# Attention with a soft mixture of experts: the sums of the weights by seven TensorE streams of a quarter of the queries per column group

## The chip, the cores and the metric

The kernel runs on one core of one Trainium2 chip. The time is the device time of one execution in microseconds; the lower the better. The engines named below are TensorE (PE, matrix products; PEld its weight loads), VectorE (DVE), ScalarE (ACT), GpSimd (POOL) and SyncE (SP, which issues the transfers, SPq).

## What is computed

Rotary attention over 8 batches of 8 heads, 576 positions, 64 channels a head, and then a soft mixture of 8 experts with 4 slots each over the 4608 tokens of 512 channels:

```python
q_rot, k_rot = rotate(q), rotate(k)
scores = scale * q_rot @ k_rot.T
attn = exp(scores - scores.max(-1))
attn = attn / (attn.sum(-1) + 1e-9)
x = (attn @ v)                       # as (4608, 512)
logits = x @ phi                     # (4608, 32)
d = softmax(logits, axis=0)          # over the tokens
slots = d.T @ x                      # 32 slots
out = softmax(logits, axis=1) @ (relu(slots @ w1[e]) @ w2[e])
```

The change concerns `attn.sum(-1)`, the sums of the weights.

## The kernel before, in words

Two heads make a pair, held in the two halves of the 128 partitions; there are 32 pairs, four to a batch. The weights of a pair (`exp` of the scores) are computed transposed, keys in the partitions and queries along the row, in nine blocks of 64 keys: `t0` to `t8`, each a TensorE product of 16 matmuls into a bank pair of the accumulator `s_ps` and a ScalarE exponential out of it (lines 220, 221). Blocks 2j and 2j+1 go to tile `a_t` j, block 8 to `a_rem`. Half the partitions of a block hold one head, half the other, and the halves change place between the first and the second 288 queries. `av0` to `av8` (line 236) multiply the values by the weights into `o_ps`, and `o_out` copies that to `xt` on ScalarE.

Ahead of that, for each pair: `load0`, `load1` bring queries and keys, `spin0`, `spin1` multiply by cosines and sines on GpSimd (line 140), `join` adds on VectorE (line 144), `high0`, `high1` cast on ScalarE, `low` takes the remainder on VectorE (line 153), `m00` to `m31` and `m_rem` find the maxima of the scores (matmuls of line 173, VectorE maxima of line 175), `m_min`, `m_turn`, `m_half`, `m_rows` turn them into a row that `t0` to `t8` subtract.

Behind it come the sums. On VectorE `add1` adds `a_t` 0 and 1 into `c_t` (line 253), `add2` adds `a_t` 2, `add3` adds the second half of `a_t` 3 (line 255). `total` (line 265) then lets TensorE sum over the partitions: four terms (the two halves of `c_t`, `a_rem`, the first half of `a_t` 3), each in a column group of its own, for each half of the queries. `total_out` copies the four partial sums to `s4` on ScalarE (line 270), `send` moves them by four transfers to `rc`, 12 queries per partition (line 276), `recip` adds the four on VectorE (line 282) and takes reciprocals, `spread` and `widen` bring them over DRAM to all partitions, and `norm` multiplies `xt` by them on GpSimd (line 299). The last two pairs go another way (`sums_turn`, `sums_wide`, `norm_wide`): TensorE turns and widens the sums. `logits`, `natural` and, once per batch, the slot sums and the softmax over slots follow two beats later; the experts come at the end.

The order of all this is written out by a table of numbers, `WHEN`: a task's number is its place in units of a quarter beat, counted from the start of its pair's beat; beat p runs all tasks sorted by their place modulo 4, each for the pair that is due. Each engine then runs its instructions in exactly that order. All TensorE results but `o_ps` go through a rotation of three bank pairs of `s_ps` (`bank2`), so a product waits until the one three places before it has been read.

Of the kernel before, what the change touches and what calls it, by code (L numbers as in the profile page):

```python
# [44 lines left out]
RC = 12  # L45
PIECE = 4
WHEN = {
    "load0": -15.9, "load1": -14.496, "spin0": -13.466, "spin1": -12.4, "join": -9.9, "high0": -9.4817, "high1":
    -9.0595, "low": -8.0, "m01": -6.5262, "m10": -5.894, "m00": -5.0601, "m11": -4.7, "load_v": -3.85, "m20": -3.771,
    "m21": -3.317, "m30": -2.9, "m31": -2.7, "m_rem": -2.6642, "m_min": -2.49, "m_turn": -1.744, "m_half": -1.667,  # L50
    "m_rows": -1.545, "t0": 0.0, "weights": 0.144, "t1": 0.2, "trickle0": 0.55, "step0": 0.5949, "t2": 1.024, "av0":
    1.159, "t3": 1.1844, "av1": 1.448, "step1": 1.516, "trickle1": 1.55, "t4": 1.9121, "t5": 1.9131, "av2": 2.25,
    "trickle2": 2.55, "add1": 2.9224, "t6": 3.0, "av3": 3.157, "av4": 3.163, "step2": 3.169, "av5": 3.179, "t7": 3.3708,
    "trickle3": 3.55, "av6": 3.6564, "t8": 3.7429, "step3": 3.7743, "add2": 4.0014, "av7": 4.504, "av8": 4.5085,
    "o_out": 4.52, "add3": 4.6009, "total": 5.54, "total_out": 5.55, "send": 5.56, "sums_turn": 6.0, "sums_wide": 6.3,
    "norm_wide": 6.4, "logits_late": 7.0, "logits_sum_late": 7.05, "recip": 7.294, "natural_late": 7.3, "spread": 7.31,
    "natural_out_late": 7.35, "widen": 7.3768, "norm": 8.706, "logits": 10.54, "logits_sum": 10.579, "stats": 11.3708,
    "natural": 11.52, "natural_out": 11.536,
# [5 lines left out]
def attn_softmoe(ctx, tc, qk, v, phi, w1, w2, cs, ident, sel, seg, out):  # L64
# [30 lines left out]
    bits = const.tile([P, 5], F32, name="bits")  # L95
    ones, warm, tiny, fold = bits[:, 0:1], bits[:, 1:2], bits[:, 2:3], bits[:, 3:5]
# [8 lines left out]
    pick = const.tile([P, NS + 1], F32, name="pick")  # L105
    nc.gpsimd.memset(pick, 0.0)
    for h in (0, 1, 2):
        nc.gpsimd.memset(pick[rows[h % 2], h:h + 1], 1.0)

    nc.vector.memset(tiny, 0.0)  # L110
    nc.vector.memset(tiny[0:32], 1e-9)
# [51 lines left out]
    def bank2():  # L163
        return ps_s.tile([P, 2, 512], F32, name="s_ps")
# [83 lines left out]
    def add(p, j):  # L248
        if j == 1:
            cts[p] = att.tile([P, 2, S], F32, name="c_t")  # L250
        c, a = cts[p], ats[p, j]
        if j < 3:
            nc.vector.tensor_tensor(out=c, in0=c if j > 1 else ats[p, 0], in1=a, op=ALU.add)  # L253
        else:
            nc.vector.tensor_tensor(out=c[:, 1], in0=c[:, 1], in1=a[:, 1], op=ALU.add)  # L255

    sg = {}
    rcs = [const.tile([96, 4, RC], F32, name=f"rc{i}") for i in range(2)]

    def total(p):  # L260
        c, r, a = cts.pop(p), rems[p], ats[p, 3]
        sg[p] = s = bank2()
        for n in range(2):
            for i, m in enumerate((c[:, 0], c[:, 1], r, a[:, 0])):
                nc.tensor.matmul(s[32 * i:32 * i + 32, n, 0:HC], lhsT=pick[:, n:n + NS], rhs=m[:, half[n]],  # L265
                                 start=True, stop=True, tile_position=(0, 32 * i))

    def total_out(p):
        s, s4 = sg[p], late.tile([P, S], F32, name="s4", bufs=1)
        nc.scalar.activation(out=s4.rearrange("p (n x) -> p n x", n=2), in_=s[:, :, 0:HC], func=AF.Identity, bias=tiny)  # L270
        sg[p] = s4

    def send(p, eng):
        s4, rc = sg.pop(p), rcs[p % 2]
        for i in range(4):
            eng.dma_start(out=rc[:, i, :], in_=s4[32 * i:32 * i + 2])  # L276
# [3 lines left out]
    def recip(p):  # L280
        rr = small.tile([P, RC], F32, name="rr", bufs=2)[0:96]
        nc.vector.tensor_reduce(out=rr, in_=rcs[p % 2].rearrange("p k x -> p x k"), axis=AX.X, op=ALU.add)
        nc.vector.reciprocal(out=rr, in_=rr)
        sg[p] = rr

    def spread(p, eng):
        rr = sg.pop(p)
        rd = dram.tile([2, S], F32, name="r_row")
        eng.dma_start(out=rd.rearrange("h (r x) -> (h r) x", x=RC), in_=rr)
        sg[p] = rd  # L290

    def widen(p, eng):
        rd = sg.pop(p)
        rbs[p] = rb = late.tile([P, S], F32, name="rb", bufs=1)
        for h in range(2):
            eng.dma_start(out=rb[rows[h]], in_=rd[h:h + 1].broadcast_to([64, S]))
# [4 lines left out]
    def sums_turn(p):  # L301
        s4 = sg.pop(p)
        t = bank2()
        for j in range(5):
            w = P if j < 4 else 64
            nc.tensor.matmul(t[0:w, 0, 2 * j:2 * j + 2], lhsT=s4[:, P * j:P * j + w], rhs=fold, start=True, stop=True)
        rn = small.tile([P, RC], F32, name="rr", bufs=2)
        nc.vector.reciprocal(out=rn[:, 0:8], in_=t[:, 0, 0:8])
        nc.vector.reciprocal(out=rn[0:64, 8:10], in_=t[0:64, 0, 8:10])
        sg[p] = rn  # L310

    def sums_wide(p):
        rn = sg.pop(p)
        sg[p] = t = bank2()
        for j in range(5):
            w = P if j < 4 else 64
            for h in range(2):
                nc.tensor.matmul(t[rows[h], j // 4, P * (j % 4):P * (j % 4) + w],
                                 lhsT=rn[0:w, 2 * j + h:2 * j + h + 1].broadcast_to([w, 64]), rhs=id_sb[0:w, 0:w],
                                 start=True, stop=True)  # L320

    def norm_wide(p):
        t, xt = sg.pop(p), xts[p]
        nc.vector.tensor_tensor(out=xt[:, 0:512], in0=t[:, 0], in1=xt[:, 0:512], op=ALU.mult)
        nc.vector.tensor_tensor(out=xt[:, 512:S], in0=t[:, 1, 0:64], in1=xt[:, 512:S], op=ALU.mult)

    def natural(p):
        b, pp = divmod(p, NP)
        if pp == 0:
            xns[b] = xp.tile([P, 5, DM], F32, name="xn")  # L330
        xt = xts[p]
        flat["n"] = t = bank2()
        for j in range(4):
            nc.tensor.transpose(t[:, 0, j * P:(j + 1) * P], xt[:, j * P:(j + 1) * P], id_sb)
        nc.tensor.transpose(t[0:64, 1, 0:P], xt[:, 512:576], id_sb)

    def natural_out(p, copy=nc.scalar.copy):
        b, pp = divmod(p, NP)
        xn, t = xns[b], flat.pop("n")
# [3 lines left out]
    def logits(p):  # L343
        b, pp = divmod(p, NP)
        xt = xts[p]
        flat["l"] = lp = bank2()[:, 0]
# [7 lines left out]
    def logits_sum(p):  # L354
        b, pp = divmod(p, NP)
        lp, lb = flat.pop("l"), l_sb[:, b % 2, :]
# [183 lines left out]
    def fast(task):  # L540
# [19 lines left out]
        "add2": lambda p: add(p, 2),  # L560
        "add3": lambda p: add(p, 3),
# [66 lines left out]
    nc.vector.memset(fold, 0.0)  # L628
    for i in range(0, P, 32):
        nc.vector.tensor_copy(out=fold[i:i + 2], in_=id_sb[i:i + 2, i:i + 2])  # L630
# [40 lines left out]
    while pending:  # L671
        step(p)
    release_stk()
    for name in ("add1", "add2", "av4", "av5", "add3", "av6", "av7", "av8", "o_out", "total", "total_out"):
        do(name, p)
# [258 lines left out]
```

## Time and profile before

| what | us |
|---|---|
| three executions | 609.35, 609.97, 616.3 |
| their median | 609.97 |
| span of the profiled execution, first to last instruction | 611.8 |

Of the profiled execution the span is the time that is known; it lies 1.8 us over the median of the three. It falls into a start (to about 45 us, until the first products with the values), 31 beats of about 15 us, one a pair, and a tail (from about 527 us: the last pair's sums, the slots, the experts' weights and the output). What the views below show is read by place: a row of a timeline has its start and its length in us, the engine, the line of the code, the operation, the tiles written and read, and how many instructions it holds.

### The profile page before, as it was taken

How to read it: one execution, taken by the hardware profiler on the slowest of the kernel's cores; microseconds unless marked ns; L12 is line 12 of the kernel's file. 1: busy time of each engine (PE TensorE's matmuls, PEld its weight loads, DVE VectorE, ACT ScalarE, POOL GpSimd, SP SyncE). 2: the span in 40 equal slices, each digit the busy share in tenths (PEclk: the TensorE clock that was granted, in tenths of full speed). 3: DMA queues.
4: the chain of work that ended last, by engine and by line, in shares of the span. 5: the costliest groups of instructions: out<-in, count | busy, mean ns of one | idle time of the engine just before them, and what ended most of it. 6: DMA issues, size and time to landing. Idle time of an engine off the chain costs nothing.

```text
span 611.8 us, 23277 instructions
## 1 busy us (share of the span) xinstructions
PE 532.9 (87%) x10064; PEld 352.1 (58%) x10064; DVE 497.0 (81%) x729; ACT 326.9 (53%) x647; POOL 315.1 (52%) x308
## 2 busy tenths in 40 slices
PE   3668999998999899989999899898898999799981
PEld 2346666656765566666656565666566666443551
DVE  6879899999998999999998999999899874322341
ACT  2145656665665565656656566565465655324441
POOL 2668498655676566647763857658654000100000
PEclk9679999999999999999999999999899999859996
DMA  7153555555555555555555555455542246649999
GB/s 260 60 195 119 175 174 173 174 174 173 174 173 174 174 174 174 173 175 174 174 173 175 173 174 174 174 174 174 171 141 62 64 130 206 206 142 350 349 376 298
DMA packets 71734, 111.63 MB, mean 182 GB/s; under 512 B 20176, under 2 KB 47568, under 8 KB 71632
## 3 DMA queue, kind: packets, MB, share of 16 engines
q1 hardware_dynamic: 71618, 110.15, 54.5%
q8 instruction: 79, 1.29, 0.9%
q14 instruction: 23, 0.19, 0.1%
q10 hardware_dynamic: 14, 0.00, 0.0%
HBM read 99.93 MB, written 9.58 MB: 179 GB/s over the span
## 4 chain that ended last, share of the span: by engine, by line
PE 35%; DVE 26%; DMA 20%; ACT 6%; SPq 5%; issue 5%; POOL 1%; DVEq 0%; ACTq 0%
PE s_ps L220 8%; PE o_ps L236 8%; DVE nm L175 7%; DMA rc<-s 7%; DMA w_exp<-in_w 6%; DVE c_t L253 6%; DVE hl L153 5%; SPq L276 4%; ACT a_t L221 3%; PE s_ps L265 3%; DMA x_in<-in_qk 3%; PE s_ps L773 3%; DMA v_in<-in_v 2%; DVE c_t L255 2%; PE s_ps L173 2%
## 5 line engine op out<-in xcount | busy, mean ns | idle before, releaser
L140 POOL TENSOR_TENSOR x_in<-x_in,cs_sb 128x288 f32<-128x288 f32 x248 | 264.9, 1101 | 63.0 <-DMA x_in<-in_qk 38.1
L221 ACT ACTIVATE a_t<-s_ps 128x576 f32<-128x576 f32 x256 | 158.9, 649 | 97.8 <-PE s_ps L220 95.9
L175 DVE TENSOR_REDUCE nm<-s_ps 128x2 f32<-128x576 f32 x256 | 187.1, 743 | 15.1 <-PE s_ps L173 14.9
L236 PE MATMUL o_ps<-a_t,v_in 64*64 64x288 f32 x2048 | 172.4, 413 | 1.0 <-ACT xt L244 0.3
L220 PE MATMUL s_ps<-hl 64*64 64x288 f16 x3456 | 155.5, 286 | 16.4 <-DVE nm L175 15.9
L220 PEld LDWEIGHTS <-hl 64*64 64x64 f16 x3456 | 104.4, 107 | 59.9 <-issue 43.8
L299 POOL TENSOR_TENSOR xt<-xt,rb 128x576 f32<-128x576 f32 x30 | 42.8, 1425 | 141.0 <-DMA rb<-r_row 104.1
L173 PE MATMUL s_ps<-hl 64*64 64x288 f16 x1024 | 82.1, 298 | 26.0 <-DVE nm L175 20.5
L220 PE MATMUL s_ps<-peak,lift 64*64 64x288 f16 x1152 | 89.1, 284 | 0.0
L236 PEld LDWEIGHTS o_ps<-a_t,v_in 64*64 64x64 f32 x2048 | 72.9, 133 | 21.0 <-issue 7.3
L173 PEld LDWEIGHTS <-hl 64*64 64x64 f16 x1024 | 45.0, 107 | 49.1 <-issue 37.7
L149 ACT CAST hl<-x_in 128x576 f16<-128x576 f32 (+1 forms) x66 | 40.1, 650 | 33.1 <-DVE x_in L144 30.3
L270 ACT ACTIVATE s<-s_ps,bits 128x576 f32<-128x576 f32 x32 | 23.7, 740 | 58.0 <-PE s_ps L265 26.3
L144 DVE TENSOR_TENSOR x_in<-x_in 128x1152 f32<-128x1152 f32 (+2 forms) x36 | 53.4, 1483 | 0.5 <-POOL x_in L140 0.4
L253 DVE TENSOR_TENSOR c_t<-c_t,a_t 128x1152 f32<-128x1152 f32 x32 | 51.6, 1611 | 0.0
L153 DVE TENSOR_TENSOR hl<-x_in,hl 128x1152 f16<-128x1152 f32 x32 | 49.5, 1546 | 1.8 <-ACT hl L149 1.8
L253 DVE TENSOR_TENSOR c_t<-a_t 128x1152 f32<-128x1152 f32 x32 | 50.6, 1582 | 0.0
L220 PEld LDWEIGHTS <-lift 64*64 64x64 f16 x1152 | 38.1, 108 | 0.6
L265 PE MATMUL s_ps<-c_t,pick 128*32 128x288 f32 x256 | 37.1, 411 | 0.0
L265 PE MATMUL s_ps<-a_rem,pick 128*32 128x288 f32 x128 | 36.9, 411 | 0.0
L265 PE MATMUL s_ps<-a_t,pick 128*32 128x288 f32 x128 | 36.9, 411 | 0.0
L221 ACT ACTIVATE a_rem<-s_ps 128x576 f32<-128x576 f32 x32 | 20.8, 651 | 17.0 <-PE s_ps L220 17.0
(183 smaller groups left out, 597.6 us busy)
## 6 DMA issues: line engine op xcount, KB each, us to landing
x_in<-in_qk SPq DMA_DIRECT2D x62, 576.0 KB
w_exp<-in_w SPq DMA_DIRECT2D x63, 512.0 KB
v_in<-in_v SPq DMA_DIRECT2D x32, 576.0 KB
rb<-r_row SPq DMA_DIRECT2D x60, 144.0 KB
out<-w_exp SPq DMA_DIRECT2D x16, 512.0 KB
rc<-s SPq DMA_DIRECT2D x120, 4.5 KB
x_in<-in_qk SPq DMA_DIRECT2D x4, 288.0 KB
out<-w_exp SPq DMA_DIRECT2D x4, 256.0 KB
```

The lines of the kernel that those rows point to most:

```text
L140: eng.tensor_tensor(out=x[:, :, c], in0=x[:, :, c], in1=cs_sb[:, :, c], op=ALU.mult)
L144: nc.vector.tensor_tensor(out=x[:, t, 0, c], in0=x[:, t, 0, c], in1=x[:, t, 1, c], op=ALU.add)
L149: nc.scalar.copy(out=halves[p][:, 1 + t, c], in_=loaded[p][:, t, 0, c])
L153: nc.vector.tensor_tensor(out=hl[:, 0:4:3], in0=x[:, :, 0], in1=hl[:, 1:3], op=ALU.subtract)
L173: nc.tensor.matmul(s[rows[c], h, 0:HC], lhsT=hl[rows[h], QH, at:at + D], rhs=hl[rows[h], KH, half[n]], start=True, stop=True)
L175: nc.vector.tensor_reduce(out=nms[p][:, n, j:8:4], in_=s[:, :, 0:HC], axis=AX.X, op=ALU.max, negate=True)
L220: nc.tensor.matmul(s[rows[h ^ n], n, 0:HC], lhsT=lhs, rhs=rhs, start=(i == 0), stop=(i == 3))
L221: nc.scalar.activation(out=weights_of(p, b).rearrange("p (n x) -> p n x", n=2), in_=s[:, :, 0:HC], func=AF.Exp, scale=SCALE)
L236: nc.tensor.matmul(o[rows[h], n, 0:HC], lhsT=vt[r, b, n], rhs=a[r, half[n]], start=(b == 0), stop=(b == KB - 1))
L253: nc.vector.tensor_tensor(out=c, in0=c if j > 1 else ats[p, 0], in1=a, op=ALU.add)
L265: nc.tensor.matmul(s[32 * i:32 * i + 32, n, 0:HC], lhsT=pick[:, n:n + NS], rhs=m[:, half[n]], start=True, stop=True, tile_position=(0, 32 ...
L299: eng.tensor_tensor(out=xts[p], in0=xts[p], in1=rbs.pop(p), op=ALU.mult)
```

## The change

`add2` and `add3` go; `add1` stays. `total` takes seven terms in place of four: the two halves of `c_t`, the four halves of `a_t` 2 and 3, and `a_rem`. The four column groups now hold four quarters of the queries (144 each), and the seven terms are added up in the accumulator. So `s4` is 128 x 144, holds finished sums, and one transfer brings them to `rc`; `recip` takes reciprocals alone. The last two pairs' way is cut to the new layout (4 executed turns in place of 10, one multiplication in place of two), and the matrix `fold`, which four VectorE copies made at the start, goes. All numbers of `WHEN` are other numbers, and the last tasks behind the loop follow the table too.

```diff
-    bits = const.tile([P, 5], F32, name="bits")
-    ones, warm, tiny, fold = bits[:, 0:1], bits[:, 1:2], bits[:, 2:3], bits[:, 3:5]
+    bits = const.tile([P, 3], F32, name="bits")
+    ones, warm, tiny = bits[:, 0:1], bits[:, 1:2], bits[:, 2:3]
...
-        if j < 3:
-            nc.vector.tensor_tensor(out=c, in0=c if j > 1 else ats[p, 0], in1=a, op=ALU.add)
-        else:
-            nc.vector.tensor_tensor(out=c[:, 1], in0=c[:, 1], in1=a[:, 1], op=ALU.add)
+        nc.vector.tensor_tensor(out=c, in0=c if j > 1 else ats[p, 0], in1=a, op=ALU.add)
...
     def total(p):
-        c, r, a = cts.pop(p), rems[p], ats[p, 3]
-        sg[p] = s = bank2()
-        for n in range(2):
-            for i, m in enumerate((c[:, 0], c[:, 1], r, a[:, 0])):
-                nc.tensor.matmul(s[32 * i:32 * i + 32, n, 0:HC], lhsT=pick[:, n:n + NS], rhs=m[:, half[n]],
-                                 start=True, stop=True, tile_position=(0, 32 * i))
+        c = cts.pop(p)
+        terms = [c[:, 0], c[:, 1]] + [ats[p, j][:, i] for j in range(N_ADD + 1, 4) for i in range(2)] + [rems[p]]
+        sg[p] = s = bank2()[:, 0, 0:QC]
+        for i, m in enumerate(terms):
+            for g in range(4):
+                n = g // 2
+                nc.tensor.matmul(s[32 * g:32 * g + 32], lhsT=pick[:, 16 * n:16 * n + NS], rhs=m[:, QC * g:QC * g + QC],
+                                 start=(i == 0), stop=(i == len(terms) - 1), tile_position=(0, 32 * g))
...
     def send(p, eng):
-        s4, rc = sg.pop(p), rcs[p % 2]
-        for i in range(4):
-            eng.dma_start(out=rc[:, i, :], in_=s4[32 * i:32 * i + 2])
+        eng.dma_start(out=rcs[p % 2], in_=sg.pop(p)[0:P:16])
...
-        nc.vector.tensor_reduce(out=rr, in_=rcs[p % 2].rearrange("p k x -> p x k"), axis=AX.X, op=ALU.add)
-        nc.vector.reciprocal(out=rr, in_=rr)
+        nc.vector.reciprocal(out=rr, in_=rcs[p % 2])
...
-        for j in range(5):
-            w = P if j < 4 else 64
-            nc.tensor.matmul(t[0:w, 0, 2 * j:2 * j + 2], lhsT=s4[:, P * j:P * j + w], rhs=fold, start=True, stop=True)
+        for u in range(2):
+            nc.tensor.matmul(t[0:HQ, 0, 8 * u:8 * u + 8], lhsT=s4[:, HQ * u:HQ * u + HQ], rhs=id_sb[:, 0:P:16],
+                             start=True, stop=True)
...
-        "add2": lambda p: add(p, 2),
-        "add3": lambda p: add(p, 3),
+        "add2": lambda p: N_ADD > 1 and add(p, 2),
...
-    nc.vector.memset(fold, 0.0)
-    for i in range(0, P, 32):
-        nc.vector.tensor_copy(out=fold[i:i + 2], in_=id_sb[i:i + 2, i:i + 2])
```

What this does to the order, engine by engine. TensorE in an ordinary beat, from the last score product ahead of the sums (line numbers shift: 265 is 267 after, 173 is 176, 220 is 223). Before:

```order
L173 MATMUL s_ps<-hl 64x288
L265 MATMUL s_ps<-c_t,pick 32x288 x2
L265 MATMUL s_ps<-a_rem,pick 32x288
L265 MATMUL s_ps<-a_t,pick 32x288
L220 LDWEIGHTS hl
```

The four rows of line 265 stand twice, once for each half of the queries. After:

```order
L176 MATMUL s_ps<-hl 64x288
L267 MATMUL s_ps<-c_t,pick 32x144 x8
L267 MATMUL s_ps<-a_t,pick 32x144 x16
L267 MATMUL s_ps<-a_rem,pick 32x144 x4
L223 LDWEIGHTS hl
```

Eight matmuls of 288 columns became 28 of 144. A little later in the same beat, before, the transpose of the maxima (line 194, `m_turn`) and the logits (348, 351) behind a product with the values (236):

```order
L236 MATMUL o_ps<-a_t,v_in 64x288 x4
L194 MATMUL s_ps<-id_sb,nm 9x128
L348 MATMUL s_ps<-xt,phi_sb 32x128 x4
L351 MATMUL s_ps<-xt,phi_sb 32x64 x4
```

And after:

```order
L239 MATMUL o_ps<-a_t,v_in 64x288 x4
L347 MATMUL s_ps<-xt,phi_sb 32x128 x4
L350 MATMUL s_ps<-xt,phi_sb 32x64 x4
L197 MATMUL s_ps<-id_sb,nm 9x128
L239 MATMUL o_ps<-a_t,v_in 64x288 x4
```

The logits moved ahead of the transpose, and a value product stands behind it. VectorE over an ordinary beat, before, from the evacuation of the logits (`l_sb`) on:

```order
L360 TENSOR_TENSOR l_sb<-s_ps,l_sb 128x192
L253 TENSOR_TENSOR c_t<-a_t 128x1152
L175 TENSOR_REDUCE nm_7258<-s_ps 128x2
L282 TENSOR_REDUCE rr<-rc_121 96x12
L283 RECIPROCAL rr<-rr 96x12
L153 TENSOR_TENSOR hl<-x_in,hl 128x2x576
L253 TENSOR_TENSOR c_t<-c_t,a_t 128x1152
L255 TENSOR_TENSOR c_t<-c_t,a_t 128x576
L187 TENSOR_REDUCE nm<-nm_7258 128x9
L144 TENSOR_TENSOR x_in<-x_in 128x2x576
```

(Maxima of line 175 stand between them.) After:

```order
L190 TENSOR_REDUCE nm<-nm_10041 128x9
L147 TENSOR_TENSOR x_in<-x_in 128x2x576
L178 TENSOR_REDUCE nm_10390<-s_ps 128x2
L255 TENSOR_TENSOR c_t<-a_t 128x1152
L359 TENSOR_TENSOR l_sb<-s_ps,l_sb 128x192
L178 TENSOR_REDUCE nm_10390<-s_ps 128x2 x2
L282 RECIPROCAL rr<-rc_120 96x12
L186 TENSOR_REDUCE nm_10390<-s_ps 128x2
L156 TENSOR_TENSOR hl<-x_in,hl 128x2x576
L178 TENSOR_REDUCE nm_10390<-s_ps 128x2 x4
```

Two of the three adds and the reduction of `rc` are gone, and the remaining add stands directly ahead of the logits' evacuation, not behind it. On ScalarE the cast `high0` now stands ahead of `m_half`; on SyncE `load1` stands behind `send`, and `m_rows` behind `load1`.

## Rows read from the trace of the kernel before

**Rows 1.** Page, part 1: busy us, share of the span and instructions of each engine

```profile
PE 532.9 (87%) x10064; PEld 352.1 (58%) x10064; DVE 497.0 (81%) x729; ACT 326.9 (53%) x647; POOL 315.1 (52%) x308
```

**Rows 2.** Timeline of ScalarE: copies of the sums; in brackets its idle time before

```profile
55.59 0.74 ACT L270 ACTIVATE s<-s_ps,bits 128x576 f32<-128x576 f32 x1 [1.62 <-PE s_ps L265]
...
471.88 0.74 ACT L270 ACTIVATE s<-s_ps,bits 128x576 f32<-128x576 f32 x1 [1.59 <-DMA v_in<-in_v]
```

**Rows 3.** Windows: length, busy of PE, PEld, DVE, ACT, POOL, TensorE clock, DMA, GB/s

```profile
55.60:471.90 416.30, 380.67 (x7937) 260.46 (x7935) 393.21 (x553) 250.03 (x491) 270.87 (x246) 1.00 0.51 167
...
471.70:485.30 13.60, 13.36 (x294) 9.28 (x291) 12.65 (x19) 8.90 (x16) 1.56 (x2) 1.00 0.24 69
485.30:500.64 15.34, 14.91 (x308) 9.79 (x305) 11.59 (x22) 8.88 (x21) 1.52 (x2) 1.00 0.38 118
...
542.50:612.00 69.50, 53.40 (x500) 26.57 (x500) 19.94 (x35) 23.84 (x50) 1.74 (x2) 0.87 0.97 319
```

**Rows 4.** Waits, 60 to 515 us: who for whom, total us, times, longest

```profile
PE s_ps L173 <- DVE nm L175: 14.2, 16, 2.1
PE s_ps L220 <- DVE nm L175: 13.2, 31, 1.4
...
DVE rr L282 <- DMA rc<-s: 7.5, 13, 1.4
```

**Rows 5.** Timeline of TensorE: transposes of a batch's logits, and what follows

```profile
504.49 0.33 PE L408 MATMUL s_ps<-id_sb,l_sb 128*128 128x128 f32 x1
...
504.86 0.47 PE L236 MATMUL o_ps<-a_t,v_in 64*64 64x288 f32 x4
```

**Rows 6.** Groups of VectorE: busy us, mean ns | idle before them, releaser

```profile
L253 DVE TENSOR_TENSOR c_t<-c_t,a_t 128x1152 f32<-128x1152 f32 x32 | 51.6, 1611 | 0.0
L253 DVE TENSOR_TENSOR c_t<-a_t 128x1152 f32<-128x1152 f32 x32 | 50.6, 1582 | 0.0
...
L255 DVE TENSOR_TENSOR c_t<-c_t,a_t 128x576 f32<-128x576 f32 x32 | 25.1, 783 | 1.4 <-ACT a_t L221 1.3
...
L282 DVE TENSOR_REDUCE rr<-rc 96x12 f32<-96x48 f32 x30 | 6.7, 224 | 7.8 <-DMA rc<-s 7.5
```

**Rows 7.** Timeline of TensorE: first two of four sets of the sums, and what follows

```profile
344.79 0.44 PE L265 MATMUL s_ps<-c_t,pick 128*32 128x288 f32 x2
...
345.06 0.41 PE L265 MATMUL s_ps<-c_t,pick 128*32 128x288 f32 x2
...
345.90 0.56 PE L220 MATMUL s_ps<-hl 64*64 64x288 f16 x12
```

**Rows 8.** Timeline of TensorE: logits (128, then 64 columns); accumulating sets of 256 columns

```profile
362.49 0.43 PE L348 MATMUL s_ps<-xt,phi_sb 128*32 128x128 f32 x8 [0.16 <-ACT a_t L221]
362.71 0.32 PE L351 MATMUL s_ps<-xt,phi_sb 128*32 128x64 f32 x8
362.96 0.32 PE L173 MATMUL s_ps<-hl 64*64 64x288 f16 x4
...
566.14 0.39 PE L797 MATMUL o_ps<-w_exp 128*32 128x256 f32 x2
...
566.36 0.39 PE L797 MATMUL o_ps<-w_exp 128*32 128x256 f32 x2
```

**Rows 9.** Waits in the ordinary beat 471.7 to 485.3

```profile
PEld s_ps L194 <- ACT a_t L221: 0.4, 1, 0.4
...
PEld o_ps L236 <- ACT xt L244: 0.4, 1, 0.4
...
PE s_ps L348 <- ACT a_t L221: 0.2, 1, 0.2
```

**Rows 10.** Timeline of SyncE's queue: the four transfers of a pair's sums

```profile
361.29 2.75 SPq L276 DMA_DIRECT2D rc<-s  x4
```

**Rows 11.** Timeline of VectorE at the start

```profile
13.11 2.86 DVE L630 COPY bits<-id_sb 2x2 f32<-2x2 f32 x4
16.00 1.42 DVE L175 TENSOR_REDUCE nm<-s_ps 128x2 f32<-128x576 f32 x2
```

## What I expect, before the result

> **What bounds the kernel now.** I read the busy shares first [rows 1]: TensorE 87%, VectorE 81%, and both fall in the tail, so a share over the whole span decides nothing. The stages do. The ScalarE copies of the sums come once per pair; the first starts at 55.59 us, that of pair 27 at 471.88 [rows 2]. So 27 steady beats take 416.3 us, 15.42 us each, and this is two thirds of the span. In that window VectorE is busy 393.2 of 416.3 us (94%, 14.56 us a beat) and TensorE 380.7 (91%, 14.10 a beat), at a full granted clock, with DMA at 0.51 [rows 3]. Both look full; which one sets the beat shows in two later beats in which GpSimd has no rotations left (busy 1.56 and 1.52 us) and VectorE runs undisturbed [rows 3]: 471.70 to 485.30 is an ordinary beat, 13.60 us, TensorE busy 13.36, VectorE 12.65; 485.30 to 500.64 holds a batch's slot sums too, 15.34 us, TensorE busy 14.91, VectorE only 11.59. There TensorE sets the beat. Of every four beats one carries slot sums, one the two transposes of a batch's logits (504.49 to 504.86, 0.37 us [rows 5]), and two neither. So a beat that TensorE alone limits is (15.34 + 13.97 + 2 x 13.60) / 4 = 14.13 us, and the 1.29 us between that and 15.42 are VectorE's doing: adds, joins and evacuations in one queue. The table of waits bears it out from TensorE's side: between 60 and 515 us, some 30 beats, TensorE's two kinds of score matmuls wait 14.2 and 13.2 us for VectorE's maxima [rows 4], 0.9 a beat. The tail from 542.50 on (DMA busy 0.97 [rows 3]) follows the attention at a fixed distance and moves with it.
>
> **The change part by part.**
>
> VectorE per beat loses the second add (1.61), the half add (0.78) and the reduction of the four partial sums (0.22) [rows 6]: 2.61 us, of 14.56 leaves 11.95. That is below any estimate of TensorE's beat, so the 1.29 us are free to go; more than them is not, because TensorE is next.
>
> TensorE's sums: 16 executed matmuls of 288 columns become 56 of 144 columns (28 in the program; every fp32 matmul runs twice, as 8 in the program are 16 in the trace). Now: four column groups run at once, a set of four starts every 0.24 us, and from the first set at 344.79 to the next work at 345.90 it is 1.11 us: four sets 0.97, change-over 0.14 [rows 7]. After: 14 sets. A 144-column set is nowhere in the trace. Nearest: two sets of 128 columns in 0.22 us, 0.11 each [rows 8], and sets of 256 columns that accumulate over terms in four column groups as the new ones do, one from 566.14 to 566.36 [rows 8]. All three come to 0.84 or 0.85 ns a column, so I take 0.12 a set: 1.68 + 0.14 = 1.82 us, 0.71 more than now. Bounds: 0.11 (the 128-column set), 0.24 (the 288-column set, as if halving brought nothing).
>
> The rows leave no room for a cost per instruction: what 128, 256 and 288 columns take is in proportion. The Trainium skill (TensorEngine Tiling (Array Packing), Instruction Overhead) says otherwise and against this change: some 60 cycles for each matmul on trn2; estimated from that page, 25 ns more for each of 14 sets, 0.35 us a beat, and the sum below would read 596.
>
> Order: the logits of an older pair now stand ahead of the transpose of the maxima (m_turn), not behind it, and the copy of the sums shrinks from 576 to 144 columns. In the ordinary TensorE-limited beat TensorE's weight load for the transpose waits 0.4 us and the logits 0.2 us for exponentials [rows 9], which themselves stand behind that 576-column copy of 0.74 us [rows 2]. Bounds: both gone (-0.6), neither (0); I take half, -0.3. The wait of the value products for the output copy (0.4 [rows 9]) stays: av8, copy and av0 keep their places.
>
> m_half moves behind the first cast (high0), which waits for VectorE's join; behind them on ScalarE stands the exponential of t6, and TensorE's next banks wait for it. On SyncE load1 moves behind the transfer of the sums and the rows of the maxima (m_rows) behind load1. I cost these at nothing: in VectorE's order join stands ahead of a maximum and the add, so it is over before the logits are evacuated, and the rotation of load1's half is due only in the next beat. If the cover is gone, the price is a wait of about the one VectorE instruction ahead, at most an add of 1.58 [rows 6] a beat; a gain I exclude, since nothing waits for these now.
>
> Transfers: four issues of 2.75 us together become one [rows 10]. VectorE's waits for them are 7.5 us in 13 times between 60 and 515 us [rows 4], part of the 1.29 already; not counted again.
>
> Start: four copies on VectorE (from 13.11 [rows 11]) go, and the first maximum (16.00) follows them with nothing in between: -2.9 us. Everything up to the first exponentials hangs on this queue; bound above 0, if GpSimd's rotation were later than the maxima.
>
> Last beats: pairs 28 to 31 are TensorE-limited already, so they pay 4 x (0.71 - 0.3) = +1.6. For the last two pairs fewer, narrower matmuls turn the sums, one of them directly behind the copy it waits for; I set this to 0, with a microsecond either way.
>
> **Sum.** A beat becomes 14.13 + 0.71 - 0.3 = 14.54 us, 0.88 less: 27 x 0.88 = -23.8. With -2.9 and +1.6 the profiled span of 611.8 becomes 586.7, 25.1 us less. The median shown, 609.97, lies 1.8 under that span; the same step down gives **585 us**.
>
> **Rivals.**
>
> *Better order:* both ScalarE waits go and the shorter copy frees more, 14.1 us a beat: 0.44 x 31 less, 571. For it: the waits named above. Against: banks are still three.
>
> *A new wait in place of the old* (nearly no change): logits and m00 share a bank of the rotation of three; logits are summed by VectorE behind the remaining add (1.58 [rows 6]), which now stands directly ahead of it, and m00 comes only four TensorE tasks later. Also m_half behind the cast. From +0.42 us a beat on (31 x 0.42 = 13) the gain falls under 2%: 598; a wait of 0.7 gives 607. For it: the rotation made such waits before; against it: VectorE has 2.6 us of slack.
>
> *A set costs more than its columns* (the other side, slower): the 64-column sets take 0.25 us for two [rows 8], 0.07 each above their columns. With that on every new set the beat has 14 x 0.07 = 0.98 more, and the time is 615, within 2%. If a 144-column set took the 0.24 us of a 288-column one, 14 x 0.12 = 1.7 a beat, 31 beats, 53 us: 638. It is slower by over 2% from 0.21 us a set on (37 us / 31 / 14 = 0.086 above 0.12). Against it: the 64-column sets are below what a set needs to be started, the 128-column ones are not, and the accumulating 256-column sets show nothing.
>
> The page's rule is a milder form of this rival (596). It needs a fixed cost that the 128- and 256-column rows don't show; 0.05 for it, within the forecast's range.
>
> That the change doesn't do what it says I exclude: the order shows the adds and three of four transfers gone in every beat.
>
> **How the numbers follow.** Forecast 0.55 (578 to 597, the page's case in it); better order 0.15 (about 571 to 578); a new wait, or a small fixed cost per set, 0.22 (598 to 615); slower through the sets 0.08 (over 622). A measurement of this kernel tells about 2% from no change, 12.2 us: faster is below 597.8, slower above 622.2. So faster 0.70, same 0.22, slower 0.08. The range: 572 to 604 leaves 0.05 below, and above it the slower case and the upper part of the new waits, 0.15.
>
> **What would show it.** Right: copies of the sums 14.5 us apart on average in steady state; starts of the sums' sets 0.12 apart, 14 of them, under 1.9 us in all; VectorE's share in the steady beats near 82%, TensorE's above 95%; VectorE's first maximum at about 13 us; one transfer of sums per pair on SyncE. Wrong: sets 0.14 or more apart; TensorE idle before m00, t7 or t0 for VectorE or a transfer; the transpose of the maxima waiting for the join; beats still at 15.

## The result, and the profile after

Four executions of the changed kernel beside four of the kernel before gave a median of 587.91 us against 611.07, a ratio of 0.962 (95% interval 0.956 to 0.969): 23 us less. The forecast was 585, in a range of 572 to 604. The span of the profiled execution is 585.4 us, 26.4 less than the 611.8 before. The sum came out; two of its terms for the beat did not, and the experiments below show which.

Page, part 1 of the kernel after (busy us, share of the span, instructions), and below it, from part 4, the share of each engine in the chain of work that ended last, first after, then before:

```profile
PE 539.7 (92%) x11356; PEld 387.5 (66%) x11356; DVE 422.7 (72%) x625; ACT 313.5 (54%) x647; POOL 298.1 (51%) x308
...
PE 85%; DVE 4%; DMA 3%; ACT 3%; issue 2%; SPq 0%; DVEq 0%; ACTq 0%
```

```profile
PE 35%; DVE 26%; DMA 20%; ACT 6%; SPq 5%; issue 5%; POOL 1%; DVEq 0%; ACTq 0%
```

Where [rows 1] had two engines near their limit, one is left: TensorE rises from 87% to 92%, VectorE falls from 81% to 72%, and the chain, which used to change between TensorE, VectorE and the transfers, now runs on TensorE almost throughout.

The copies of the sums, which [rows 2] used as the clock of the beats (name of the instruction, count, shortest/median/longest in ns, first and last start), and three windows of the kernel after (length, busy us of PE, PEld, DVE, ACT, POOL, granted TensorE clock, DMA share, GB/s), to be laid beside [rows 3]:

```profile
L272 ACT ACTIVATE s<-s_ps,bits x32: 380/380/382, 51.2 to 502.8; 128x144 f32<-128x144 f32 x32
```

```profile
51.20:446.46 395.26, 389.70 (x9017) 292.89 (x9016) 332.57 (x471) 238.23 (x490) 257.99 (x249) 1.00 0.55 177
446.46:502.78 56.32, 54.92 (x1240) 39.46 (x1232) 25.90 (x46) 30.46 (x66) 4.50 (x5) 1.00 0.42 126
...
518.28:585.40 67.12, 49.60 (x491) 25.58 (x480) 20.04 (x35) 23.29 (x48) 1.73 (x2) 0.91 1.00 329
```

The copies of pairs 0 and 27 start at 51.20 and 446.46: 27 steady beats of 14.64 us, against 15.42. In them TensorE is busy 98.6% (91% before) and VectorE 84% (94% before). The span of 26.4 us less falls apart by these marks: 4.4 ahead of the first copy (55.59 to 51.20), 21.0 in the 27 steady beats (416.3 to 395.3), 1.4 given back in the last four (54.9 to 56.3), 2.4 behind the last copy.

Waits of the kernel after between 60 and 480 us (who for whom, total us, times, longest): the largest of TensorE's own, two of its weight loads, one of VectorE:

```profile
PE s_ps L223 <- issue: 2.3, 6, 0.6
```

```profile
PEld o_ps L239 <- ACT xt L247: 9.0, 29, 0.3
PEld s_ps L333 <- ACT a_t L224: 8.3, 24, 0.3
```

```profile
DVE nm L178 <- PE s_ps L176: 52.0, 89, 2.2
```

The 14.2 and 13.2 us that TensorE's score products waited for VectorE's maxima [rows 4] are gone, and the sign has turned: VectorE now waits 52 us for score products. The weight load of the product with the values still waits 0.3 us a beat for the output copy, as the prediction left it.

The new sums on TensorE, in an ordinary beat (start, length, engine, line, what, count):

```profile
341.03 0.70 PE L267 MATMUL s_ps<-c_t,pick 128*32 128x144 f32 x16
341.54 1.16 PE L267 MATMUL s_ps<-a_t,pick 128*32 128x144 f32 x32
342.52 0.43 PE L267 MATMUL s_ps<-a_rem,pick 128*32 128x144 f32 x8
```

```profile
342.88 0.56 PE L223 MATMUL s_ps<-hl 64*64 64x288 f16 x12
```

Fourteen sets begin within 1.85 us up to the next product; 12 sets lie between 341.03 and 342.52, 0.124 us each. The prediction had 0.12 and 1.82.

### The profile page after: what moved, and what is told of

It reads as the page before. It is cut to its first block, busy times and chain, and to the rows that moved or that the text cites. A ratio compares the mean times of both kernels' runs of the same rounds, so it can differ in the third digit from the quotient of the medians.

```text
span 585.4 us, 25500 instructions
## 1 busy us (share of the span) xinstructions
PE 539.7 (92%) x11356; PEld 387.5 (66%) x11356; DVE 422.7 (72%) x625; ACT 313.5 (54%) x647; POOL 298.1 (51%) x308
## 4 chain that ended last, share of the span: by engine, by line
PE 85%; DVE 4%; DMA 3%; ACT 3%; issue 2%; SPq 0%; DVEq 0%; ACTq 0%
PE o_ps L239 27%; PE s_ps L223 24%; PE s_ps L267 10%; PE s_ps L176 5%; PE s_ps L333 3%; PE s_ps L773 2%; ACT xt L247 2%; PE s_ps L347 2%; DMA w_exp<-in_w 1%; DVE nm L178 1%; PE o_ps L797 1%; PE s_ps L397 1%; PE s_ps L197 1%; DMA out<-w_exp 1%; PE s_ps L797 1%
## 5 line engine op out<-in xcount | busy, mean ns | idle before, releaser
L143 POOL TENSOR_TENSOR x_in<-x_in,cs_sb 128x288 f32<-128x288 f32 x248 | 248.0, 1033 | 96.2 <-DMA x_in<-in_qk 73.5
L178 DVE TENSOR_REDUCE nm<-s_ps 128x2 f32<-128x576 f32 x256 | 184.7, 754 | 60.9 <-PE s_ps L176 59.4
L239 PE MATMUL o_ps<-a_t,v_in 64*64 64x288 f32 x2048 | 183.4, 413 | 3.0 <-issue 0.5
L223 PE MATMUL s_ps<-hl 64*64 64x288 f16 x3456 | 162.9, 286 | 3.0 <-issue 2.1
L223 PEld LDWEIGHTS <-hl 64*64 64x64 f16 x3456 | 111.1, 107 | 37.7 <-issue 18.5
L223 PE MATMUL s_ps<-peak,lift 64*64 64x288 f16 x1152 | 103.0, 284 | 0.2 <-issue 0.2
L176 PE MATMUL s_ps<-hl 64*64 64x288 f16 x1024 | 88.3, 291 | 7.4 <-ACT a_t L224 3.7
L223 PEld LDWEIGHTS <-lift 64*64 64x64 f16 x1152 | 46.6, 107 | 2.0 <-issue 0.8
L272 ACT ACTIVATE s<-s_ps,bits 128x144 f32<-128x144 f32 x32 | 12.2, 380 | 52.1 <-PE s_ps L267 42.5
L267 PE MATMUL s_ps<-a_t,pick 128*32 128x144 f32 x1024 | 37.2, 286 | 0.0
L267 PEld LDWEIGHTS s_ps<-a_t,pick 128*32 128x32 f32 x1024 | 31.6, 110 | 0.0
L186 DVE TENSOR_REDUCE nm<-s_ps 128x2 f32<-128x576 f32 x32 | 24.2, 755 | 10.1 <-PE s_ps L184 9.0
L339 ACT COPY xn<-s_ps 128x512 f32<-128x512 f32 x31 | 18.1, 585 | 23.1 <-PE s_ps L334 23.1
```

The costliest lines, as they stand in the source:

```text
L143: eng.tensor_tensor(out=x[:, :, c], in0=x[:, :, c], in1=cs_sb[:, :, c], op=ALU.mult)
L176: nc.tensor.matmul(s[rows[c], h, 0:HC], lhsT=hl[rows[h], QH, at:at + D], rhs=hl[rows[h], KH, half[n]], start=True, stop=True)
L178: nc.vector.tensor_reduce(out=nms[p][:, n, j:8:4], in_=s[:, :, 0:HC], axis=AX.X, op=ALU.max, negate=True)
L223: nc.tensor.matmul(s[rows[h ^ n], n, 0:HC], lhsT=lhs, rhs=rhs, start=(i == 0), stop=(i == 3))
L239: nc.tensor.matmul(o[rows[h], n, 0:HC], lhsT=vt[r, b, n], rhs=a[r, half[n]], start=(b == 0), stop=(b == KB - 1))
L267: nc.tensor.matmul(s[32 * g:32 * g + 32], lhsT=pick[:, 16 * n:16 * n + NS], rhs=m[:, QC * g:QC * g + QC], start=(i == 0), stop=(i == len(t ...
```

## Experiments

Each run is the changed kernel with the edit shown. Medians and ratios are against the kernel before, run on the same chip; the ratio of the changed kernel itself, 0.962, is what they are to be compared with. Since the parts of a run that have nothing to do with the edit vary too, I also give the mean of the 27 steady beats, read as above: 15.42 us before, 14.64 after. How far that mean can be trusted shows in the last run, whose steady beats, all but the last of them, have the same program as the changed kernel: 14.79. So 0.15 us a beat, 4 us in all, is nothing. The mean before has such a chance part too. Its longest beat, in the row below, took 19.45 us: TensorE waited 0.83 and 1.41 us for VectorE's maxima, and then the granted clock was 0.50 (1.2 GHz) from 436 to 438 us. Without that beat the mean before is 15.26.

```profile
422.36:441.81 19.45, 16.66 (x316) 11.29 (x312) 17.61 (x25) 10.02 (x24) 14.20 (x15) 0.91 0.59 202
```

Of the long lines of the table the diffs below show mostly the entries that differ.

### The sums alone, and the order alone

The first run has the new sums and the table of positions of the kernel before (without the two adds that are gone):

```diff
-    "load0": -15.6934, "spin0": -14.3205, "load1": -13.2037, "spin1": -12.6294, "join": -9.9457, "high0": -9.686,
...
+    "load0": -15.9, "load1": -14.496, "spin0": -13.466, "spin1": -12.4, "join": -9.9, "high0": -9.4817, "high1":
...
```

> The changed kernel with the table of positions of the kernel before (the sums, the one transfer, the shorter start as changed). Theory T (the work taken from VectorE brings the gain, the new order a small part, 0.3 us a beat): 588 + 27 x 0.3 + 0.3 x 4, about 597 us; steady beat 14.9 us. Rival O (the new order brings most of it, the sums cost TensorE what they save VectorE): 610 us or more. Rival N (the order brings nothing): 586 to 590.

Measured: 609.0 us, ratio 0.989 (0.983 to 0.995), steady beat 15.29 us.

The second run has the old sums (three adds, four terms, four transfers, the fold matrix) and the new table, with a place for the third add; the second add stands at 3.50, where the new table has it:

```diff
+    "add3": 4.4,
...
+        for n in range(2):
+            for i, m in enumerate((c[:, 0], c[:, 1], r, a[:, 0])):
```

> The changed kernel with the sums of the kernel before: three adds on VectorE (the half add at 4.4), four terms on TensorE, four transfers, four fold copies at the start; the new positions for everything else. T: VectorE keeps 14.6 us a beat, so the beat stays near 15.4 minus at most 0.3: 601 to 611 us. Rival O (the order is the gain): 585 to 592 us, beat 14.6.

Measured: 619.1 us, ratio 1.005 (1.002 to 1.009), steady beat 15.51 us; the time lies above both expectations.

So neither half of the change brings the gain. The sums alone take 0.13 us off a beat, the order alone adds 0.09, neither more than a profile varies by; both together take off 0.78. In the whole time the sums alone are worth 1.1%, and the order alone loses 0.5%, both by a little more than their intervals. The prediction's theory (sums nearly all, order 0.3) falls with the first run, the rival (order alone, with the adds in these places) with the second. Windows of the 27 steady beats, of the first run and of the second:

```profile
54.68:467.47 412.79, 396.97 (x9017) 292.88 (x9017) 334.20 (x471) 243.26 (x490) 257.51 (x246) 1.00 0.50 168
```

```profile
55.48:474.14 418.66, 382.38 (x7937) 262.33 (x7937) 392.83 (x552) 248.87 (x490) 285.35 (x249) 1.00 0.51 167
```

In the first, VectorE is as free as in the changed kernel (334.20 of 412.79 us), TensorE's 9017 matmuls are the same, and yet TensorE is idle 15.8 us, not 5.6, and its busy time is 7.3 us longer (the rows overlap: a matmul of the new sums is shown 0.29 us long while sets start 0.124 us apart, so a short wait counts as busy). The time goes in many small pieces (waits of the first run, 60 to 480 us; "issue" means that the trace shows no releaser):

```profile
PE s_ps L175 <- DVE nm L177: 4.7, 6, 1.3
...
PEld L175 <- issue: 13.5, 47, 1.3
PEld L222 <- issue: 11.1, 36, 1.2
PEld s_ps L196 <- ACT a_t L223: 10.5, 24, 0.4
PEld o_ps L238 <- issue: 8.7, 35, 1.2
```

Taking work from VectorE in the old order frees VectorE, and TensorE goes on losing time. Where, these rows tell only in part: 4.7 us end with a maximum, most of the others name no releaser, and waits of weight loads, which run beside the matmuls, stand in the kernel after as well. My reading is that a bank of the rotation comes back when its reader's turn in its queue comes, whatever that engine's load is. The runs below show this at single places (the remainder's maximum, the spare add); for the old order as a whole it is not shown. In the second run VectorE is full (94%), and TensorE waits for maxima as before. One of these waits, 60 to 480 us, is for the remainder's maximum:

```profile
PE s_ps L224 <- DVE nm L187: 15.9, 23, 1.5
```

It is the wait that the spare add at the same place, 3.50, makes below. So the second run shows that the new table brings nothing with the second add there; a table with other places for the old adds was not run.

### What the table's change consists of

Two runs put pieces of the old table back. The pair of tasks that the prediction had priced:

```diff
-    "m_turn": -1.4,
+    "m_turn": -1.45,
```

> The changed kernel with one pair of tasks swapped back: the transpose of the maxima (m_turn) ahead of the logits. By the order term as the prediction set it (0.3 us a beat from this swap and the shorter copy): up to 31 x 0.3 = 9 us more, 592 to 597 us. If this swap is worth nothing: 586 to 590. If it carries what the old table costs as a whole (21 us): 603 to 609.

Measured: 591.2 us, ratio 0.962 (0.956 to 0.968), steady beat 14.74 us. The swap is worth nothing that can be seen. The transpose waits for the exponential again, as before (9.9 us in 25 times from 60 to 480 us), but the rest takes that up.

The remainder's scores and maximum, which the new table has 5 us earlier in a pair's life, a move that the prediction did not name:

```diff
-    "m_rem": -4.0891,
+    "m_rem": -2.72,
```

> The changed kernel with the remainder's scores and maximum (m_rem) put back behind m31, where the old table has them, some 5 us later in a pair's life, so that the minimum over the maxima and the transpose follow it closely. If this move carries what the old table costs: 600 to 609 us. If not: 586 to 592 us.

Measured: 597.2 us, ratio 0.973 (0.966 to 0.980), steady beat 14.87 us, 0.23 more than the changed kernel. The time lies between the two expectations, and the intervals overlap; but there is a new wait, at the place of the edit. It is that of TensorE's sums, whose bank the remainder's maximum still holds (waits of TensorE and of its weight loads, 60 to 480 us):

```profile
PE s_ps L267 <- DVE nm L186: 4.3, 22, 0.2
...
PEld s_ps L267 <- DVE nm L186: 10.8, 22, 0.5
```

Then the table in two halves: in one run the middle of the beat (from `join` and `m10` to `t7`) is new and the rest old, in the other the reverse. Some entries of the first, and then of the second:

```diff
-    "m_rem": -4.0891, "t8": 4.1933, "spread": 8.0448, "widen": 8.109
+    "m_rem": -2.6642, "t8": 3.7429, "spread": 7.31, "widen": 7.3768
```

> The changed kernel's sums with the old positions, except in the middle of the beat (from join and m10 to t7: logits, m_turn, m_half, the casts, add1, the sum of the logits, m00, t6, m11, natural), which stands as in the new table. The old table as a whole gave 609, the new one 588. If the middle carries the gain of the order (the bank of the logits is asked back by t6 in the old order, by m00 three TensorE tasks later in the new one): 588 to 595 us. If the rest carries it (m_rem earlier, t8 behind the turn of the beat): 602 to 609. If both halves are needed together: 605 to 612 here and in the run with the rest new.

```diff
-    "add1": 2.4214, "logits": 10.5611, "m_turn": -1.4, "m00": -4.9584, "m_rows": -0.383
+    "add1": 2.9224, "logits": 10.54, "m_turn": -1.744, "m00": -5.0601, "m_rows": -1.545
```

> The other half: the changed kernel's sums, the middle of the beat as in the old table, the rest as in the new one. If the middle carries the gain: 602 to 609 us. If the rest carries it: 588 to 595. If the two halves add up: the two runs together lie 21 us below twice 609, and by the 9 us that m_rem's place was worth, this one is at 595 to 602.

Measured: with the rest new, 596.3 us, ratio 0.972 (0.969 to 0.975), steady beat 14.83: of the 0.65 us that the order is worth with the new sums (15.29 against 14.64), the rest alone brings 0.46. Whether the middle brings the other 0.19 stays open. With the middle new, 723.2 us, ratio 1.177 (1.171 to 1.182), the largest loss of the study. That run says nothing on the middle, since the mixture made a wait that neither table has. From its waits, 60 to 480 us, for TensorE and for SyncE's queue:

```profile
PE s_ps L223 <- DMA peak<-mr: 70.5, 23, 4.3
```

```profile
SPq L288 <- DVE rr L282: 89.1, 22, 5.1
SPq L295 <- DMA r_row<-rr: 26.6, 22, 2.6
```

The order of SyncE's queue in one beat of that run (`spread`, `widen`, `m_rows`), and the product that follows on TensorE:

```profile
300.55 0.33 SPq L288 DMA_DIRECT2D r_row<-rr  x1
302.92 1.31 SPq L295 DMA_DIRECT2D rb<-r_row  x2
304.32 0.57 SPq L206 DMA_DIRECT2D peak<-mr  x1
```

```profile
306.26 0.51 PE L223 MATMUL s_ps<-peak,lift 64*64 64x288 f16 x4 [3.42 <-DMA peak<-mr]
```

The old table has `spread` and `widen` (lines 288, 295) at places 3.31 and 3.38 of a beat, the new one has `m_rows` at 3.62, behind them in this mixture. So the row of maxima waits until the reciprocals of an older pair are there and have come back from DRAM, and `t0`, which subtracts that row, waits 3.1 us in 23 beats. In neither whole table does `m_rows` stand right behind them: the old one has it ahead of both, the new one has both at the very start of the beat. A transfer that depends on nothing late became late by its neighbour in the queue. The prediction had costed the moves on SyncE at nothing; that holds for the whole new table, in which TensorE does not wait for these transfers between 60 and 480 us.

### What VectorE has to spare

An add that nobody reads, at 3.50 in the beat, where a second add has its place:

```diff
-        "add2": lambda p: N_ADD > 1 and add(p, 2),
+        "add2": idle_add,
...
+        nc.vector.tensor_tensor(out=spare, in0=ats[p, 1], in1=ats[p, 2], op=ALU.add)
```

> The changed kernel with one more add per pair on VectorE, into a spare tile that nobody reads, at the place of the second add; TensorE's work as in the changed kernel. T: VectorE goes from 12.3 to 13.9 us in a beat that TensorE holds at 14.64: between no change and + 0.4 us a beat, 588 to 600 us. Rival V (VectorE sets the beat): + 31 x 1.58, 637 us.

Measured: 612.3 us, ratio 0.999 (0.995 to 1.002), steady beat 15.43 us. That is dearer than expected, between the two expectations: 0.79 us a beat for an add of 1.72 us, though VectorE had 62.7 of 395.3 us idle, 2.3 a beat. The whole gain of the change is gone. The window (the same 9017 matmuls), and the wait that appeared, 60 to 480 us:

```profile
53.42:469.99 416.57, 394.28 (x9017) 291.56 (x9014) 363.46 (x498) 240.65 (x490) 291.93 (x249) 1.00 0.52 167
```

```profile
PE s_ps L223 <- DVE nm L186: 16.5, 25, 1.4
```

One beat shows how. TensorE finishes the remainder's scores (L184), VectorE is in the spare add, then takes their maximum (L186), and the product that gets that bank starts (L223):

```profile
351.64 0.65 PE L239 MATMUL o_ps<-a_t,v_in 64*64 64x288 f32 x6
...
353.77 0.56 PE L223 MATMUL s_ps<-hl 64*64 64x288 f16 x12 [0.50 <-DVE nm L186]
```

```profile
351.03 1.94 DVE L260 TENSOR_TENSOR spare<-a_t 128x1152 f32<-128x1152 f32 x1
352.89 0.21 DVE L287 RECIPROCAL rr<-rc 96x12 f32<-96x12 f32 x1
353.03 0.69 DVE L186 TENSOR_REDUCE nm<-s_ps 128x2 f32<-128x576 f32 x1
```

The last of the remainder's scores start just ahead of 351.64. Without the spare add VectorE could take the maximum at once (in the changed kernel it sits waiting for these scores 15 times between 60 and 480 us, 0.60 us each), but now comes to it at 353.03, and TensorE waits until 353.77.

The same place with an add that is of use, which spares TensorE two terms:

```diff
-N_ADD = 1
+N_ADD = 2
```

> The changed kernel with N_ADD = 2: a second full add on VectorE (1.58 us a pair), five terms on TensorE instead of seven (4 sets of 0.1225 = 0.49 us a pair less). If TensorE alone sets the beat as long as VectorE stays below it (T, strictly): 14.64 - 0.49 = 14.15 us a beat, 573 us. If two engines that are both nearly full cost each other time, as in the kernel before (VectorE 13.9 of 14.15): beat 14.7 to 15.1, 590 to 602 us. Rival V (VectorE still sets the beat in the changed kernel): + 31 x 1.58, 630 us or more.

Measured: 593.8 us, ratio 0.966 (0.961 to 0.970), steady beat 14.83 us, with the same wait (14.6 us in 24 times). The 0.49 us that TensorE saves pays for most of the 0.79. Cut into halves, in front of two maxima for which VectorE waits:

```diff
+    "add2a": 3.03, "add2b": 3.5015,
...
+        nc.vector.tensor_tensor(out=c[:, i], in0=c[:, i], in1=a[:, i], op=ALU.add)
```

> The changed kernel with the second add on VectorE, cut into two half adds of 0.79 us: one ahead of m00's maximum (VectorE idle 0.55 us there in an ordinary beat), one ahead of the remainder's maximum (0.60 idle); TensorE sums five terms, 0.49 us a pair less. If the idle places take up most of it (P): 0.2 to 0.5 us of delay against 0.49 gained, 580 to 590 us. If VectorE's length decides (V): as with the second add in one piece, 592 to 596.

Measured: 588.5 us, ratio 0.959 (0.954 to 0.963), steady beat 14.69 us: not to be told from the changed kernel, and 0.14 us a beat below the add in one piece, at the edge of what a profile varies by. VectorE is as busy as with the add in one piece, but the wait for the remainder's maximum is down to 5.8 us in 7 times, and another, for m00's, has come:

```profile
PE s_ps L223 <- DVE nm L186: 5.8, 7, 1.1
...
PE s_ps L223 <- DVE nm L178: 4.7, 10, 0.7
```

This suggests that an add's price is that of its place. Both adds moved ahead, the first to the place ahead of m10's maximum, where VectorE was idle 0.99 us in one ordinary beat:

```diff
-    "add1": 2.4214, "add2": 3.5015, "logits_sum": 10.9713
+    "add1": 2.08, "add2": 2.62, "logits_sum": 10.6
```

> The changed kernel with two adds on VectorE and five terms on TensorE, as with two adds before, but at other places: the first add moves ahead of the maximum of m10, before which VectorE sits idle 0.99 us in an ordinary beat, the sum of the logits moves up, and the second add follows it; none stands right ahead of the remainder's maximum. Theory P (an add costs where TensorE waits for the maximum behind it, not by VectorE's busy time): TensorE's 0.49 us a beat less come through, 31 x 0.49 = 15 off 588: 573 to 578 us. Theory V (VectorE's throughput decides: 13.9 us in a beat of 14.2): as with two adds at the old place, 590 to 596 us.

Measured: 601.0 us, ratio 0.979 (0.974 to 0.985), steady beat 15.09 us, above both expectations. My placement was worse than the old place: the same work costs 0.26 us a beat more there. VectorE and GpSimd in two successive beats of that run:

```profile
337.53 1.34 DVE L147 TENSOR_TENSOR x_in<-x_in 128x1152 f32<-128x1152 f32 x1
338.79 2.57 DVE L255 TENSOR_TENSOR c_t<-a_t 128x1152 f32<-128x1152 f32 x1
341.29 0.75 DVE L178 TENSOR_REDUCE nm<-s_ps 128x2 f32<-128x576 f32 x1
...
352.15 2.56 DVE L147 TENSOR_TENSOR x_in<-x_in 128x1152 f32<-128x1152 f32 x1
354.63 1.35 DVE L255 TENSOR_TENSOR c_t<-a_t 128x1152 f32<-128x1152 f32 x1
```

```profile
338.41 1.74 POOL L299 TENSOR_TENSOR xt<-xt,rb 128x576 f32<-128x576 f32 x1 [4.51 <-DMA rb<-r_row]
...
352.08 1.41 POOL L299 TENSOR_TENSOR xt<-xt,rb 128x576 f32<-128x576 f32 x1 [1.47 <-ACT a_t L224]
```

A sum of two tiles takes 1.34 us here, and 2.57 where GpSimd's multiplication has begun just ahead of it: in the first beat it is the add, in the second the join. With the add in that place m10's maximum comes at 341.29, and the next product that wants its bank waits 0.50 us; over 60 to 480 us it is 16.0 us in 19 times. The idle time was smaller than the add, and the 0.99 us were not typical: in 27 beats of the changed kernel, from 60 to 450 us, VectorE's idle time at that place is 0 in ten and 0.45 us on average. And the place has a neighbour that can make the add twice as long.

### What TensorE has to spare

Four more terms in the sums, with zero weights, 8 sets more a pair:

```diff
+        for i in range(4):
+            for g in range(4):
+                nc.tensor.matmul(s[32 * g:32 * g + 32], lhsT=nil, rhs=rems[p][:, QC * g:QC * g + QC],
...
```

> The changed kernel with four more terms in the sums, with zero weights so that they add nothing: 8 more sets of 144 columns on TensorE per pair, 8 x 0.1225 = 0.98 us. T (TensorE sets the beat of the changed kernel): 31 x 0.98 = 30 us more, 615 to 620 us. If the beat is set by waits between the engines and TensorE has slack inside it: 590 to 605 us. If a set costs more than its columns when more of them stand in a row: over 625 us.

Measured: 621.1 us, ratio 1.012 (1.008 to 1.016), that is, by the ratios, 30 us over the changed kernel; steady beat 15.71 us, 1.07 more for 0.98 of work. TensorE sets the beat of the changed kernel, and nothing in it hides sums.

Last, the sums of the last five pairs back on VectorE, which has few maxima left there:

```diff
-N_ADD = 1
+N_ADD = {27: 2, 28: 3, 29: 3, 30: 3, 31: 2}
```

> The changed kernel with the sums of the last five pairs put back on VectorE, which has no scores to wait for there (TensorE's busy share in the last four beats 54.9 of 56.3 us, VectorE's 25.9): two adds for pairs 27 and 31, three for 28 to 30, so 4 + 3 x 8 + 4 sets of sums fewer... in all 2 x 0.49 + 3 x 0.98 = 3.9 us less on TensorE. T: 584 us. If VectorE's adds delay the chain of the last pair: 588 or more.

Measured: 588.4 us, ratio 0.960 (0.957 to 0.963). The stretch from the copy of pair 27 to that of pair 31 takes 55.7 us instead of 56.3; of the 3.4 us of sums that TensorE is spared in it (pair 27's 0.49 lie ahead of it), 0.6 arrive. Waits for VectorE's maxima (1.6 us in two), which the changed kernel does not have there, take a part; the rest I did not settle. No version of the twelve is shown to beat the changed kernel.

## Why the prediction was right, and where it was not

**The bound.** That TensorE is next behind VectorE was right: the window after (98.6% busy), the chain (85%) and the run with four more terms (slope 1.1) all say so.

**The sums on TensorE.** 0.12 us a set and 1.82 us in all were predicted, 0.124 and 1.85 measured. The rival in which a set costs more than its columns did not come. The Trainium skill (TensorEngine Tiling (Array Packing), Instruction Overhead) gives some 60 cycles for each matmul; by the prediction's estimate from it, which adds them to each set, the sums would take 2.17 us. The trace does not agree with that reading: 1.85.

**VectorE's 1.29 us.** This step failed: "so the 1.29 us are free to go", whatever the order. Its base, 14.13 us, was read from two beats in which GpSimd has no rotations left and, in the second, VectorE has no join and no remainder to take. An add takes 1.35 us there, one row from each beat below, and 1.58 or 1.61 on average [rows 6]; TensorE sat idle 0.24 and 0.43 us even so [rows 3].

```profile
474.72 1.35 DVE L253 TENSOR_TENSOR c_t<-a_t 128x1152 f32<-128x1152 f32 x1
488.32 1.35 DVE L253 TENSOR_TENSOR c_t<-a_t 128x1152 f32<-128x1152 f32 x1
```

The 15.42 that it was set against has the one beat of 19.45 in it, worth some 0.15 us. In the old order the new sums give 15.29 us a beat where the step has 14.84. VectorE was relieved, to 12.38 us a beat in that run (2.18 less, of the 2.61 predicted), and is idle for a fifth of it, but 0.45 us a beat stayed all the same. So VectorE's load is not what holds the rest; that its turn in the order is, the runs show at the places named above, and for the rest it stays open.

**The order, -0.3.** Mis-sized, and for the wrong reason. With the new sums the order is worth 0.65 us a beat, with the old ones, in the places that they had there, nothing (+0.09). The swap that I priced brings nothing that can be seen by itself (14.74), while the half of the table in which the remainder's maximum, `t8` and the transfers of the reciprocals stand brings 0.46; the place of the remainder's maximum alone is worth 0.23. I had looked for the rows in which a task had plainly changed sides, and had read past the remainder's maximum, whose bank the sums then take. The two errors, 0.45 too much from the sums and 0.35 too little from the order, cancelled to 0.1 us a beat: 14.54 predicted, 14.64 measured. The right total is not evidence for its two terms.

**"VectorE has 2.6 us of slack"**, the argument against a new wait, was right in size (2.3 measured) and wrong as cover: 1.72 us of it, in front of one maximum, cost 0.79 us a beat, which the spare add shows. The rival of a new wait behind the remaining add did not come; why not, no run here tests.

**Moves costed at nothing.** That of `m_rows` on SyncE makes no wait of TensorE's in the whole new table, and 3 us a beat as soon as `spread` and `widen` do not move with it.

**Start.** -2.9 was predicted, and -2.8 came. The first maximum starts at 13.17, against 16.00 [rows 11]:

```profile
13.17 4.07 DVE L178 TENSOR_REDUCE nm<-s_ps 128x2 f32<-128x576 f32 x6
```

The first copy of the sums comes 4.4 us earlier, so 1.6 more were won between. With the new sums in the old order the first maximum is as early (13.19), but the first copy comes at 54.68, only 0.9 earlier: here too the order had to let the gain through.

**Last beats.** +1.6 predicted, +1.4 measured.

**Tail.** 0 predicted, "with a microsecond either way", and -2.4 measured, from the last copy of the sums to the end. The rows of the first products with the experts' weights, of the kernel after and of the kernel before, divide it:

```profile
516.80 2.34 PE L773 MATMUL s_ps<-w_exp,slot_t 128*32 128x512 f32 x18 [0.38 <-DVE slot_t L761]
```

```profile
542.51 4.48 PE L773 MATMUL s_ps<-w_exp,slot_t 128*32 128x512 f32 x18 [0.38 <-DVE slot_t L761]
```

From the last copy (at 502.78 and 526.77) to the start of these products it is 14.02 us after and 15.74 before, 1.7 less; from their start to the end 68.6 and 69.3, 0.7 less. The first part goes with the edit: the run with the old sums and the new order has 15.51 there, and the runs with the new sums have 10.7 to 14.5. So the shorter way of the last two pairs' sums, which the prediction set to 0, is worth about a microsecond or more. In the second part the 18 matmuls of the rows take 2.34 us after and 4.48 before, and the granted clock decides that. Windows over their start, after and before:

```profile
516.80:519.00 2.20, 2.20 (x24) 0.70 (x28) 0.00 (x0) 1.03 (x3) 0.00 (x0) 1.00 0.35 116
```

```profile
542.51:546.00 3.49, 3.49 (x20) 0.86 (x24) 0.00 (x0) 0.55 (x2) 0.00 (x0) 0.50 0.05 15
```

It is 1.00 after (2.4 GHz), and 0.50 before (1.2 GHz). Ahead of that TensorE did much the same in both: from the last copy of the sums on, 10.70 of 13.80 us busy at a mean of 0.63 after, 12.16 of 15.50 at 0.64 before. Nor does the clock go with the edit: with the old order it is 1.00 there (2.34 us), with the transpose first 0.50 (4.48 us). Of the 2.1 us between the two rows at most 0.7 reach the end; those I count as no part of the change's effect.

## What to carry to other kernels

Where engines hand each other a few banks in a fixed order, relief of one engine and the order can be one change, as here: a two-by-two of both, the old with the new, tells what neither a busy share nor the sum of two terms can. Look in it for places that the mixture brings and that cost time of their own, as the second add at 3.50 and `m_rows` behind `widen` did here. Before work goes onto an engine that "has slack", look up what stands behind it in that engine's queue and who waits for that; idle time elsewhere in the beat does not pay for it. And a queue of transfers is passed in order: one that waits makes all behind it late.

## What the runs showed of the hardware

In the two beats shown, a VectorE sum of two tiles that began while GpSimd multiplied two tiles took 2.56 or 2.57 us instead of 1.34, longer by 1.22, a little less than what was then left of GpSimd's instruction (1.36 and 1.34 us). The Trainium skill says so (SBUF — State Buffer, Who interferes with whom): a VectorE instruction with two inputs from SBUF and a GpSimd instruction that reads SBUF exclude each other, and the second to issue waits for the first to end. The rows above agree: 352.08 + 1.41 + 1.34 is 354.83, and the join ended at 354.71. The steady windows fit the other side of it: with the spare add GpSimd's 249 instructions are busy for 291.93 us, in the changed kernel for 257.99. For the prediction it means that the mean of 1.58 us for an add [rows 6] was no duration of the add, but a mean over its neighbours.
